# Attention values as 64x64 quarters, in two halves around the next quad's first scores

## The chip, the cores and the metric

The kernel runs on one core of a Trainium2 chip. The metric is device time in microseconds for one execution; the median of several runs is quoted. Beside it there is one profiled execution with its trace. A core has five engines that run their own instruction streams and wait for each other through semaphores: TensorE (PE in the profile; its weight loads are PEld), VectorE (DVE), ScalarE (ACT), GpSimd (POOL) and SyncE (SP), which issues most transfers here.

## The reference

Attention with normalised queries and keys, and then a feed-forward block over its output, all in fp32:

```
q, k, v: (8, 12, 448, 64)
q_n, k_n = rmsnorm(q, g_q), rmsnorm(k, g_k)
scores   = matmul(q_n, k_n^T) / sqrt(64)
attn     = softmax(scores)
x        = matmul(attn, v), laid out as (3584, 768)
h        = x @ w_in                      # 768 -> 1024
solu     = h * softmax(h)
out      = layernorm(solu) * g_ln @ w_out  # 1024 -> 768
```

The weights arrive as float64 and are converted to fp32 in the kernel.

## The kernel before

The work has three stages: attention (to 316 us of the trace), the first product of the feed-forward block, and the second. The change lies in the attention stage, in `fast_path`. `general_path` is a fallback that does not run on these inputs.

**Quads and pairs.** The 96 heads (8 batches of 12) are handled four at a time, as 24 quads; a quad m is two pairs, a = 2m and b = 2m + 1, and a pair is two heads h = 0 and 1 stacked on 128 partitions, 64 each. The 448 keys of a head are three blocks of 128 (kc = 0 to 2) and a rest of 64. Everything is kept transposed: keys on partitions, queries along the free dimension.

**Scores.** `scores(n, kc)` (L804) makes four products of 64x64 weights with 448 columns: two row halves of the array are the two heads, two column halves are the two halves of a key block. The two heads go to two PSUM banks of one tile `s` (pool `ps_t`, tag "t", three buffers of two banks). ScalarE then takes one exponential over both heads (L802), E. `scores_last(m)` (L818) does the rest of 64 keys for both pairs at once. There is no subtraction of a maximum; the gains are bounded by a check instead.

**Values.** Each pair has one PSUM bank `o` (tag "o", two buffers): 64 partitions for each head. `values_last(m)` (L850) begins both banks with the rest of 64 keys, in four products of 64x64: row half i works for pair i. `values(n)` (L863) adds the three key blocks of one pair: 128 keys on all rows of the array, 64 columns for each head, so two products fill the array (shape 128x64). `values(a)` and `values(b)` follow each other. An fp32 product appears in the trace as two matmul instructions.

**Sums and division.** `add` (L836) and `add_more` (L844) add blocks of E on VectorE and GpSimd; `sums(m)` (L874) makes the sums over keys with products against ones, 128x32, into a tile `sm` of tag "t". `inverse(m)` (L896) turns them into reciprocals on VectorE, with copies on GpSimd (L910). `divide(m)` (L912) multiplies `o` by them: two transposes (L917) and two products (L918); the first frees the bank of pair a, the second that of pair b. `store_x` sends the result to DRAM.

**Norms.** For the quad after the next, `squares` (L669, ScalarE) and `row_sums` (L676, VectorE) run; `fold_sums` (L684, GpSimd) joins quarters of partitions. For the next quad, `rsqrt_seed` (L693: L697 and L698 on ScalarE), `rsqrt_step` (VectorE), `normalise` (L709, GpSimd), `qk_transpose` (L720, VectorE) and `gain` (L725, ScalarE, scales q by the gains) prepare `qkT`, which the scores read.

**Weight conversion.** In the quads of `steps_at`, 4 to 10, 12, 14, 16, 18 and 20 (twelve in all), `begin(m)` (L1344) runs the first step of one conversion: `low_bits` (L534), two instructions on ScalarE, of which L536 reads what L535 wrote. `step(m - 1)` runs the second step, on VectorE, one quad later.

**The order.** Inside `manual_schedule` each engine executes its instructions in the order in which the code calls them; the framework adds the semaphore waits. The loop over quads (from L1385) writes that order by hand. `unit(f)` (L1317) calls f and moves a counter on by one unit; `later(n, g)` (L1314) calls g when n more units have passed, so that `divide(m)` is called after the first unit of the next quad. For a quad from 2 to 21 the order on TensorE is: scores of a (three), the last scores, scores of b (three), `values_last`, `values(a)`, `values(b)`, `sums`. On ScalarE: seven exponentials, two squares, two gains, in the quads of `steps_at` L535 and L536, and L697 and L698 for the next norms. The calls behind the last scores read:

```
            if next2:
                squares(a + 4)
                squares(b + 4)
                row_sums(a + 4)
            if next1:
                gain(a + 2)
                gain(b + 2)
```

and, further on, `unit(outputs)` (values_last and values(a)), `step(m - 2)`, `begin(m)`, `step(m - 1)`, loads of weights, and `unit(lambda: values(b))`.

Of the kernel before, what the change touches and what calls it, by code (L numbers as in the profile page):

```python
# [366 lines left out]
def fast_path(  # L367
# [24 lines left out]
    nc = tc.nc  # L392
    B, H, S, D = q.shape
    DM, DFF = moe_w_in.shape
    P = 128
    NJ = S // P
    NB = S // 32
    NP = H // 2
    NQ = B * NP // 2
# [16 lines left out]
    first, middle, banks_in = ExitStack(), ExitStack(), ExitStack()  # L416
# [201 lines left out]
    st = {}  # L618
    quads = {}
# [49 lines left out]
    def squares(n):  # L669
        d = st[n]  # L670
        d["sq"] = work.tile([P, 2 * NB, 32], FP32, tag="sq", name="sq", bufs=2)
        nc.scalar.activation(d["sq"].rearrange("p (s b) d -> p s (b d)", s=2), d["qk"], AF.Square)  # L672
# [20 lines left out]
    def rsqrt_seed(d):  # L693
        ss = d["ss"]
        p, w = ss.shape
        y = d["y"] = small.tile([P, 4 * NB], FP32, tag="ny", name="ny", bufs=2)[0:p, 0:w]
        nc.scalar.activation(y, ss, AF.Ln, scale=1.0 / D, bias=eps[0:p])  # L697
        nc.scalar.activation(y, y, AF.Exp, scale=-0.5)  # L698

    def rsqrt_step(d):  # L700
        y, ss = d["y"], d["ss"]
        p, w = ss.shape
        x = small.tile([P, 4 * NB], FP32, tag="nx", name="nx", bufs=2)[0:p, 0:w]
        nc.vector.tensor_scalar(x, ss, -0.5 / D, -0.5e-6, OP.mult, OP.add)
        nc.vector.tensor_tensor(x, x, y, OP.mult)
        nc.vector.tensor_tensor(x, x, y, OP.mult)
        nc.vector.scalar_tensor_tensor(y, x, 1.5, y, OP.add, OP.mult)
# [17 lines left out]
    def gain(n):  # L725
        d = st[n]
        nc.scalar.activation(d["qkT"][:, 0], d["qkT"][:, 0], AF.Copy, scale=gcol[:, KF : KF + 1])
# [72 lines left out]
    def exponentials(d, kc, s):  # L800
        d["E", kc] = big_tile("E")[:, 0 : 2 * S].rearrange("p (h t) -> p h t", h=2)
        nc.scalar.activation(d["E", kc], s[:, :, 0:S], AF.Exp)  # L802

    def scores(n, kc):  # L804
        d = st[n]
        s = ps_t.tile([P, 2, 512], FP32, tag="t", name="s")

        for c in range(0, P, D):
            for h in range(2):
                hh = slice(h * D, (h + 1) * D)  # L810
                keys = slice(NJ * c + kc, NJ * (c + D - 1) + kc + 1, NJ)
                nc.tensor.matmul(  # L812
                    s[c : c + D, h, 0:S], d["qkT"][hh, 1, keys], d["qkT"][hh, 0, :],
                    start=True, stop=True,
                )
        exponentials(d, kc, s)
# [16 lines left out]
    def on_vector(m):  # L833
        return m >= NQ - 2

    def add(n):  # L836
        d = st[n]
        d["es"] = work.tile([P, 2, S], FP32, tag="es", name="es")
        nc.vector.tensor_tensor(d["es"], d["E", 0], d["E", 1], OP.add)  # L839

    def whole(n):
        return on_vector(n // 2) or n % 2 == 0

# [6 lines left out]
    def values_last(m):  # L850

        d = quads[m]
        for i in range(2):
            o = st[2 * m + i]["o"] = ps_t.tile([P, S], FP32, tag="o", name="o", bufs=2)
        for h in range(2):
            for i in range(2):
                pp = slice(i * D, (i + 1) * D)
                nc.tensor.matmul(  # L858
                    st[2 * m + i]["o"][h * D : (h + 1) * D, :], d["vl"][pp, h], d["E", NJ][pp, h],
                    start=True, stop=False,  # L860
                )

    def values(n):  # L863


        d = st[n]
        for kc in range(NJ):
            for h in range(2):
                nc.tensor.matmul(  # L869
                    d["o"][h * D : (h + 1) * D, :], quads[n // 2]["v"][:, n % 2 + 2 * h, kc], d["E", kc][:, h],  # L870
                    start=False, stop=(kc == NJ - 1),
                )
# [48 lines left out]
    def store_x(m):  # L921
        b, hp = divmod(2 * m, NP)
        xo = quads.pop(m)["xo"]
        rows = xd[b].rearrange("(g h i d) t -> h d g i t", h=2, i=2, d=D)
        for h in range(2):
            nc.sync.dma_start(rows[h][:, hp // 2], xo[h * D : (h + 1) * D])
# [5 lines left out]
    banks = []  # L932
# [384 lines left out]
    def unit(f, steps=4):  # L1317
        nonlocal now
        f()
        now += steps  # L1320
        due = [x for x in todo if x[0] <= now]
        todo[:] = [x for x in todo if x[0] > now]
        for _, g in sorted(due, key=lambda x: x[0]):
            g()
# [40 lines left out]
    with tc.manual_schedule():  # L1365
# [19 lines left out]
        for m in range(NQ):  # L1385
            a, b = 2 * m, 2 * m + 1

            def outputs():
                values_last(m)
                values(a)  # L1390


            next1 = m + 1 < NQ
            next2 = m + 2 < NQ
            next3 = m + 3 < NQ
            early = m > 0 and next1

            def norms_next():
                rsqrt_seed(norms[m + 1])
                rsqrt_step(norms[m + 1])  # L1400
                normalise(a + 2)
                normalise(b + 2)

            if m == 0:
                unit(lambda: scores(a, 0))
                normalise_rows(1, 0)
                normalise_rows(1, 1)
                unit(lambda: scores(a, 1))
                unit(lambda: scores(a, 2))
                squares_half(3, 0, True)  # L1410
                for s in range(2):
                    transpose_rows(1, s)
                    take_rows(1, s)
                squares(2)
                squares_half(3, 1, False)
                add(a)
                add_more(a)
                row_sums(2)
                unit(lambda: scores_last(m))
                row_sums(3)  # L1420
                fold_sums(1)
                unit(lambda: scores(b, 0))
                unit(lambda: scores(b, 1))
                add(b)
                norms_next()
                unit(lambda: scores(b, 2))
                squares(4)
                row_sums(4)
                squares(5)
                unit(outputs)  # L1430
                qk_transpose(2)
                gain(2)
                row_sums(5)
                qk_transpose(3)
                fold_sums(2)
                unit(lambda: values(b))
                unit(lambda: sums(m))
                inverse(m)
                later(1, lambda m=m: divide(m))
                continue  # L1440
            if early:
                norms_next()
            for x in joins_at.get(m, ()):
                combine_in(x)
            if next1:
                load_v(m + 1)
            if m == 1:
                load(m + 3)
            unit(lambda: scores(a, 0))
            if m == 1:  # L1450
                gain(3)
            store_x(m - 1)
            if early:
                qk_transpose(a + 2)
                if next3 and m > 1:
                    load(m + 3)
            unit(lambda: scores(a, 1))
            unit(lambda: scores(a, 2))
            unit(lambda: scores_last(m))
            unit(lambda: scores(b, 0))  # L1460
            unit(lambda: scores(b, 1))
            if early:
                qk_transpose(b + 2)
            add(a)
            if not on_vector(m):
                add_more(a)
            unit(lambda: scores(b, 2))
            if next2:
                squares(a + 4)
                squares(b + 4)  # L1470
                row_sums(a + 4)
            if next1:
                gain(a + 2)
                gain(b + 2)
            if next2:
                row_sums(b + 4)
                fold_sums(m + 2)
            add(b)
            if on_vector(m):
                add_more(a)  # L1480
                add_more(b)
            unit(outputs)
            step(m - 2)
            begin(m)
            step(m - 1)
            if m - 1 in sets:
                load_next()
            if m == 2:
                load_next()
                load_next()  # L1490
            if m == 3:
                norm_gain()
            unit(lambda: values(b))
            if m == NQ - 1:
                block_sums(0, 0)
                block_sums(0, 1)
                load_x(1)
            unit(lambda: sums(m))
            inverse(m)
            if next1:  # L1500
                later(1, lambda m=m: divide(m))
            if m == NQ - 2:
                load_x(0)
                sizes(0)
# [62 lines left out]
        for n in range(NS):  # L1567
            base = period * n
            for i, name in enumerate(ORDER):
# [4 lines left out]
                x = HALVES[name][0]  # L1574
# [118 lines left out]
```

## Time and profile before

| | us |
|---|---|
| runs, median of 3 | 802.53 (802.07 to 803.22) |
| profiled execution, its time | 803.36 |
| span of its trace | 801.6 |
| attention stage, up to the first product of L990 | 316.3 |
| one quad, m = 12 (from values_last to values_last) | 12.52 |
| TensorE busy in 18 to 316 us | 295.92 of 298.00 |
| VectorE, ScalarE, GpSimd busy there | 253.84, 227.26, 214.45 |

The profile's first part gives busy time and share of each engine, the second its share in 40 slices and the granted TensorE clock, the fourth the chain that ended last. A line of the timeline has the start in us, the duration from the first start to the last end, the engine, the source line, the operation, the tile written and those read, the part of the array in rows*columns for products, the shape, the number of merged instructions, and in brackets idle time ahead of it with what ended it. Ends of matmuls are modelled and overlap the next start, so differences of starts tell the pace.

### The profile page before, as it was taken

Reading aid. Unit: us, or ns where it says so; the run is one execution under the profiler, and the core shown is the slowest. Engines: PE = TensorE matmul, PEld = TensorE weight load, DVE = VectorE, ACT = ScalarE, POOL = GpSimd, SP = SyncE. Lnnn points to the kernel's source line nnn. Section 1 sums busy time; section 2 is a strip of 40 time slices with the busy share of each in tenths; the row PEclk is TensorE's granted clock in tenths of the full one; section 3 lists DMA queues with packets and bytes.
Section 4 is the critical chain, followed back from the end, with each engine's and each line's share of the span. In section 5 each row is a group of like instructions: output and inputs, shape, how many; then the busy total and the mean of one; then the engine's idle time right before and its main releaser. Section 6 shows DMA issues by size and latency. Waiting matters only on the chain.

```text
span 801.6 us, 14271 instructions
## 1 busy us (share of the span) xinstructions
PE 788.1 (98%) x4854; PEld 462.7 (58%) x4854; DVE 613.7 (77%) x1202; ACT 472.2 (59%) x783; POOL 523.1 (65%) x664
## 2 busy tenths in 40 slices
PE   8999999999999999999999999999999999999997
PEld 4344444444444443444444444444789999999996
DVE  6787989989888896488878666777896776866945
ACT  6677878878778774376766544444515455464420
POOL 2666777778876784234456467668698777877861
PEclk9999999999999999999999999999999999999999
DMA  9878889897787832445554435552757457366312
GB/s 169 164 174 156 175 194 186 194 189 161 169 157 169 158 102 75 136 117 155 152 146 131 113 98 141 142 137 52 190 167 233 147 183 264 123 221 223 112 61 83
DMA packets 269598, 122.68 MB, mean 153 GB/s; under 512 B 187596, under 2 KB 254668, under 8 KB 269516
## 3 DMA queue, kind: packets, MB, share of 16 engines
q1 hardware_dynamic: 254332, 111.78, 55.9%
q10 hardware_dynamic: 15184, 9.90, 4.5%
q8 instruction: 40, 0.66, 0.3%
q14 instruction: 42, 0.34, 0.1%
HBM read 84.94 MB, written 36.70 MB: 152 GB/s over the span
## 4 chain that ended last, share of the span: by engine, by line
PE 87%; DVE 3%; DMA 2%; SPq 2%; POOL 2%; ACT 2%; issue 1%; DVEq 0%; ACTq 0%; POOLq 0%
PE A L1205 14%; PE A L990 13%; PE o L869 12%; PE s L812 12%; PE B L990 8%; PE B L1205 7%; PE C L990 4%; PE sm L891 4%; PE D L990 4%; PE C L1205 3%; PE s L825 2%; PE o L858 2%; SPq L636 1%; DMA xg<-xd 1%; ACT E L802 1%
## 5 line engine op out<-in xcount | busy, mean ns | idle before, releaser
L802 ACT ACTIVATE E<-s 128x896 f32<-128x896 f32 x168 | 138.8, 937 | 8.3 <-PE s L812 7.8
L812 PE MATMUL s<-qkT 64*64 64x448 f32 x1152 | 120.1, 545 | 1.0 <-ACT qkT L786 0.6
L869 PE MATMUL o<-E,v 128*64 128x448 f32 x576 | 113.8, 543 | 0.0
L1079 POOL TENSOR_TENSOR he<-he,mhalf 128x1 f32<-128x1 f32 x28 | 27.4, 977 | 102.5 <-DVE he L1078 97.4
L812 PEld LDWEIGHTS s<-qkT 64*64 64x64 f32 x1152 | 48.0, 163 | 59.4 <-ACT E L802 29.3
L1205 PE MATMUL A<-w_out,sums 128*128 128x192 f32 x392 | 79.9, 327 | 1.6 <-POOL sums L1185 1.2
L869 PEld LDWEIGHTS o<-E,v 128*64 128x64 f32 x576 | 39.1, 137 | 72.2 <-issue 68.0
L1205 PE MATMUL B<-w_out,sums 128*128 128x192 f32 x392 | 79.8, 326 | 0.5 <-DVE P L1267 0.5
L713 POOL TENSOR_TENSOR qkn<-qk,ny 128x896 f32<-128x896 f32 x46 | 77.2, 1699 | 3.8 <-DMA qk<-in_q_dram 1.5
L848 POOL TENSOR_TENSOR es<-es,E 128x896 f32<-128x896 f32 x22 | 46.4, 2110 | 48.8 <-ACT sq L672 34.0
L990 PE MATMUL B<-w_in,xsum 128*128 128x512 f32 x168 | 76.7, 592 | 0.0
L990 PE MATMUL A<-w_in,xg 128*128 128x512 f32 x168 | 74.6, 593 | 0.0
L1061 ACT ACTIVATE u<-h,hmax 128x1024 f32<-128x1024 f32 x28 | 32.2, 1148 | 66.8 <-DVE hmax L1055 66.8
L1205 PEld LDWEIGHTS A<-w_out,sums 128*128 128x128 f32 x392 | 66.1, 190 | 2.4 <-POOL sums L1185 1.5
L1205 PEld LDWEIGHTS B<-w_out,sums 128*128 128x128 f32 x392 | 66.2, 190 | 0.8 <-DVE P L1267 0.8
L839 DVE TENSOR_TENSOR es<-E 128x896 f32<-128x896 f32 x48 | 53.9, 1124 | 2.7 <-ACT E L802 2.7
L990 PEld LDWEIGHTS B<-w_in,xsum 128*128 128x128 f32 x168 | 31.9, 190 | 40.2 <-issue 39.2
L990 PEld LDWEIGHTS A<-w_in,xg 128*128 128x128 f32 x168 | 31.8, 190 | 40.1 <-issue 39.3
L690 POOL COPY ss<-part 32x56 f32<-32x56 f32 x92 | 47.0, 511 | 5.9 <-DVE part L680 1.4
L680 DVE TENSOR_REDUCE part<-sq 128x28 f32<-128x896 f32 x46 | 47.9, 1080 | 3.9 <-ACT sq L672 1.6
L723 DVE STREAM_TRANSPOSE qkT<-qkn 128x896 f32<-128x896 f32 x46 | 48.4, 1087 | 0.0
L563 POOL TENSOR_TENSOR w_out<-w_out 128x384 f32<-128x384 f32 x44 | 45.0, 1028 | 1.3
(153 smaller groups left out, 1651.0 us busy)
## 6 DMA issues: line engine op xcount, KB each, us to landing
ur<-ud SPq DMA_DIRECT2D x60, 256.0 KB, 4.6
ud<-ub SPq DMA_DIRECT2D x112, 128.0 KB, 2.3
xd<-xo SPq DMA_DIRECT2D x48, 224.0 KB, 3.0
qk<-in_q_dram SPq DMA_DIRECT2D x92, 112.0 KB, 3.1
qk<-in_k_dram SPq DMA_DIRECT2D x92, 112.0 KB, 3.0
v<-in_v_dram SPq DMA_DIRECT2D x24, 384.0 KB, 4.3
out_dram<-P SPq DMA_DIRECT2D x19, 384.0 KB, 4.2
raw<-in_moe_w_in_dram SPq DMA_DIRECT2D x12, 512.0 KB, 5.3
```

What stands on the lines that cost most here:

```text
L563: nc.gpsimd.tensor_tensor(o, p, q, OP.subtract)
L680: nc.vector.tensor_reduce(norms[m]["part"][:, i], st[n]["sq"], AX, OP.add)
L690: e.tensor_copy(ss[g * 32 : g * 32 + 32], part[o * 32 : o * 32 + 32])
L713: e.tensor_tensor(d["qkn"].rearrange("p (s b) d -> p s b d", s=2), d["qk"].rearrange("p s (b d) -> p s b d", d=32), y.rearrange("p (s b) - ...
L723: nc.vector.transpose(d["qkT"].rearrange("p s t -> p (s t)"), d["qkn"].rearrange("p b d -> p (b d)"))
L802: nc.scalar.activation(d["E", kc], s[:, :, 0:S], AF.Exp)
L812: nc.tensor.matmul(s[c : c + D, h, 0:S], d["qkT"][hh, 1, keys], d["qkT"][hh, 0, :], start=True, stop=True,)
L839: nc.vector.tensor_tensor(d["es"], d["E", 0], d["E", 1], OP.add)
L848: e.tensor_tensor(d["es"], d["es"], d["E", 2], OP.add)
L869: nc.tensor.matmul(d["o"][h * D : (h + 1) * D, :], quads[n // 2]["v"][:, n % 2 + 2 * h, kc], d["E", kc][:, h], start=False, stop=(kc == NJ ...
L990: nc.tensor.matmul(k[bank], a[:, c], w_in[i][:, c], start=begin and c == 0, stop=c == HD - 1, skip_group_check=not begin,)
L1205: nc.tensor.matmul(k[bank], a[:, c].rearrange("p a i -> p (a i)"), w_out[:, area, i, c], start=begin and c == 0, stop=c == KC - 1, skip_gr ...
```

## The change

For the quads 1 to 22 (`halved`), the three key blocks of both pairs are multiplied together in 64x64 quarters: of each key block the row half that holds one half of the keys works for pair a while the other works for pair b. `values_part(m, 0)` does this for one assignment of halves to pairs, `values_part(m, 1)` for the exchanged one. [...] `turn(m)` puts a no-op on ScalarE that waits for the last product of part 0, and the first product of part 1 waits for the no-op. Between the two parts stand the next quad's first scores, `scores(a + 2, 0)`, which leave the head of that quad's own order. `gain(a + 2)` is called ahead of the squares, `gain(b + 2)` behind the no-op.

```diff
+    def halved(m):
+        return 0 < m < NQ - 1
+
...
+    def values_part(m, part):
+        first = None
+        for kc in range(NJ):
+            for i in range(2):
+                d = st[2 * m + i]
+                pp = slice((part ^ i) * D, (part ^ i) * D + D)
+                for h in range(2):
+                    x = nc.tensor.matmul(
+                        d["o"][h * D : (h + 1) * D, :], quads[m]["v"][pp, i + 2 * h, kc], d["E", kc][pp, h],
+                        start=False, stop=(part == 1 and kc == NJ - 1),
+                    )
+                    first = first or x
+        if part == 0:
+            quads[m]["half"] = x
+        else:
+            behind(first, quads[m]["turn"])
+
+    def behind(x, y):
+        tc.add_manual_dep(
+            getattr(x, "ins", x), getattr(y, "ins", y).name,
+            mybir.DependencyInfo(mybir.DependencyClass.Sync, mybir.DependencyReason.DATA),
+            reason="row tiles change banks",
+        )
+
+    def turn(m):
+        x = quads[m]["turn"] = nc.scalar.nop()
+        behind(x, quads[m]["half"])
...
             def outputs():
                 values_last(m)
-                values(a)
+                if halved(m):
+                    values_part(m, 0)
+                else:
+                    values(a)
...
-            unit(lambda: scores(a, 0))
             if m == 1:
+                unit(lambda: scores(a, 0))
                 gain(3)
+            else:
+                unit(lambda: scores(a, 1))
             store_x(m - 1)
             if early:
                 qk_transpose(a + 2)
                 if next3 and m > 1:
                     load(m + 3)
-            unit(lambda: scores(a, 1))
+            if m == 1:
+                unit(lambda: scores(a, 1))
             unit(lambda: scores(a, 2))
...
             unit(lambda: scores(b, 2))
+            if next1:
+                gain(a + 2)
             if next2:
                 squares(a + 4)
                 squares(b + 4)
                 row_sums(a + 4)
-            if next1:
-                gain(a + 2)
-                gain(b + 2)
...
-            unit(lambda: values(b))
+            if halved(m):
+                turn(m)
+                gain(b + 2)
+                unit(lambda: scores(a + 2, 0))
+                unit(lambda: values_part(m, 1))
+            else:
+                unit(lambda: values(b))
```

In the changed kernel's instruction streams the no-op stands on ScalarE directly behind L535 and L536 in the quads of `steps_at`, and directly behind the second square in the others (in quad 3 behind a copy of a gain column, L477); the order on VectorE, GpSimd and of SP's transfers is that of before.

## The prediction

> **What bounds the kernel now.** I read the page first. TensorE is busy in nearly every slice at full clock, and the chain that ended last lies on it for 87% of the span: whatever lengthens or shortens TensorE's own sequence in the attention stage moves the end.
>
> ```profile
> PE 788.1 (98%) x4854; PEld 462.7 (58%) x4854; DVE 613.7 (77%) x1202; ACT 472.2 (59%) x783; POOL 523.1 (65%) x664
> PEclk9999999999999999999999999999999999999999
> PE 87%; DVE 3%; DMA 2%; SPq 2%; POOL 2%; ACT 2%; issue 1%; DVEq 0%; ACTq 0%; POOLq 0%
> ```
>
> Then TensorE's timeline of one quad (m = 12; start, duration, line). Quads 1 to 21 repeat it every 12.52 us without idle time, but for quad 3 (12.82, one transpose more).
>
> ```profile
> 165.24 2.52 PE L812 MATMUL s<-qkT 64*64 64x448 f32 x24
> 167.58 0.93 PE L825 MATMUL s<-qkT 64*64 64x448 f32 x8
> 168.33 2.43 PE L812 MATMUL s<-qkT 64*64 64x448 f32 x24
> 170.59 0.93 PE L858 MATMUL o<-E,vl 64*64 64x448 f32 x8
> 171.44 4.73 PE L869 MATMUL o<-E,v 128*64 128x448 f32 x24
> 176.11 0.96 PE L891 MATMUL sm<-E,ones 128*32 128x224 f32 x16
> 176.89 0.94 PE L891 MATMUL sm<-es,ones 128*32 128x224 f32 x16
> 177.76 0.64 PE L812 MATMUL s<-qkT 64*64 64x448 f32 x4
> ```
>
> Read starts, not durations, which overlap. L825 to L812: 0.75 us for eight instructions, which start four together, so 0.376 per filling of the array. The values take 12 steps of two: 12 x 0.376 = 4.51. Both shapes fill the array, and the change wins nothing in products. Where the shape changes, a start comes late: L858 to L869 is 0.86 instead of 0.75 (0.11), L869 to L891 is 4.67 instead of 4.51 (0.16), and L891 and L812 give up the rest, 0.02, 0.11 and 0.08. In the single instructions: 64x64 to 128x64 costs 0.16, 128x64 to 128x32 0.12, 128x32 to 64x64 0.20.
>
> Then ScalarE and VectorE over the same quad, because the change hangs a wait on the one and pulls a product ahead of the other.
>
> ```profile
> 166.32 5.78 ACT L802 ACTIVATE E<-s 128x896 f32<-128x896 f32 x7
> 171.92 1.84 ACT L672 ACTIVATE sq<-qk 128x896 f32<-128x896 f32 x2
> 173.60 1.27 ACT L727 ACTIVATE qkT<-qkT,gcol 128x448 f32<-128x448 f32 x2
> 174.72 0.82 ACT L535 ACTIVATE tmp<-raw,seven 128x512 f32<-128x512 uint32 x1
> 175.57 0.63 ACT L536 ACTIVATE tmp<-tmp 128x512 int32<-128x512 f32 x1
> 177.34 0.34 ACT L697 ACTIVATE ny<-ss,eps 128x56 f32<-128x56 f32 x1 [1.14 <-POOL ss L691]
> ```
>
> From starts: 0.80 per exponential, 0.84 per square, 0.56 per gain, 0.85 from L535 to L536. L536 reads what L535 wrote and waits for its end. Twelve quads (steps_at) have this conversion pair.
>
> ```profile
> 165.38 0.42 DVE L902 STREAM_TRANSPOSE r<-sm 128x224 f32<-128x224 f32 x1 [0.48 <-PE sm L891]
> 169.23 0.62 DVE L918 TENSOR_TENSOR xo<-o,r 128x448 f32<-128x448 f32 x1
> ```
>
> Call t the first score product after the sums (165.24). The second division, which frees the bank of pair b, ends at 169.85 = t + 4.62; L858 needs the bank at t + 5.35. There are 0.73 us to spare.
>
> [...]
>
> ```profile
> 435.74 0.63 ACT L535 ACTIVATE tmp<-raw,seven 128x384 f32<-128x384 uint32 x1
> 436.41 0.52 ACT L536 ACTIVATE tmp<-tmp 128x384 int32<-128x384 f32 x1
> ```
>
> Behind this L536 stands the semaphore wait of L1085, for a VectorE product that ended at 435.39. It ran at 436.412, 6 ns after L536 began, not at 435.4; two more behind L536 (382.35, 396.92) did the same. So the sequencer goes ahead of the engine, but not past an instruction whose own semaphore is missing. The measurement decides.
>
> **The change part by part**, for the 22 quads m = 1 to 22; quads 0 and 23 keep the old form. The order of VectorE, GpSimd and of SP's transfers, compared between the two built programs, is the same; only TensorE's and ScalarE's differ.
>
> *Quarters for values.* Twelve fillings before, twelve after, at 0.376 as L858 shows: nothing. The change of shape into values (0.16) goes; the one into sums stays, now from 64x64, a pair that the trace doesn't have. Bounds: 0.10 to 0.20, the smallest first step and the largest whole switch seen; I take 0.13, near the one into the same 128x32. Saved per quad 0.28 - 0.13 = 0.15 (0.08 to 0.18), in 22 quads **-3.4 us** (-4.0 to -1.8). The quarters are issued with two columns of one row tile together, where L858 alternates rows. L869 also alternates columns at 0.376, so I cost it at nothing[...].
>
> *Squares behind gain(a+2), gain(b+2) behind the no-op.* The first gain starts 0.80 after the last exponential (t + 5.88), ends at t + 6.6, and is needed at t + 7.6. The squares come 0.56 later than they would; the first ends by t + 7.44, and VectorE, busy with the addition at L839 until then, reduces it no sooner than at t + 7.72 today. gain(b+2) and the early exponential take 1.4 us that ScalarE idles through now (1.14 us before L697, 0.87 after it). Nothing. Were that room gone, the price would be what exceeds it.
>
> *One score product pulled ahead.* From t to L858 there are now six score products, not seven: t + 4.60. The division that frees bank b still ends at t + 4.62, since its chain starts at the sums. With 0.05 us from an end on another engine to TensorE (L825 at 306.21 after an exponential that ended at 306.16) and 0.05 until the step is regular again, about 0.1 us is lost (0 to 0.3). The cover of 0.73 is gone. Behind the waiting L858 all values and sums are queued. It counts in the ten quads without conversion, **+1.0**; in the others it is part of the next wait. Quad 2 has its divisions 0.37 us later than the rest: **+0.3**, once.
>
> *The no-op.* The second half may start when the no-op has run, and the no-op needs the first half's end and its turn in ScalarE's order. TensorE reaches the second half at t + 4.60 + 0.75 (L858) + 2.26 (half) + 0.75 (scores) = t + 8.36. In the ten quads without conversion the first half ends at t + 7.8 (last start 7.23, and 0.54), and the answer is back by t + 7.9: hidden by the scores. In the twelve with conversion the no-op stands behind L535 and L536: last exponential at t + 5.08, gain + 0.80, squares + 0.56, L535 after 2 x 0.84 at t + 8.12, L536 and so the no-op at t + 8.97, TensorE at t + 9.05. Wait 0.69, and 0.05 until the step is regular: 0.74 (0.5 to 0.9). Queued behind it: the second half, the sums, the next scores. ScalarE, VectorE and GpSimd fed by them just move with it. 12 x 0.74 = **+8.9 us** (6.0 to 10.8).
>
> Sum: -3.4 + 1.0 + 0.3 + 8.9 = +6.8. The profiled execution (803.36, span 801.6) would become 810.2; it lies 0.8 above the median of the runs. On 802.53 that gives **809.3 us**.
>
> **The rivals.** (A) The above, 809.3; with the ends of its terms 805 to 813. (B) The no-op is not held[...]: only the 0.1 us of bank b stays, in all 22 quads: -3.4 + 2.2 + 0.3, 801.7. [...] against it the three waits behind L536. (C) Faster: the no-op passes, and the bank is free in time because the margin is a few hundredths: -3.4, 799.1. It decides if the no-op runs by t + 8.2 and the division ends by t + 4.55. (D) The issue order of the quarters shows a weight load in each step[...]. For it: L858's rows alternate; against it: L869.
>
> **How the numbers follow.** A 0.80, B 0.09, C 0.06, D 0.05. About 0.2% (1.6 us) is what a measurement can tell from no change: below 800.9 C and a little of B, within it B's rest and A's lowest end, above it A and D: 0.07, 0.10, 0.83. A's own range, 804 to 813, holds 0.75 of all; reaching to B gives 801.5 to 813.0.
>
> **What would show it.** In the new profile: value products at steps of 0.376 in 64x64 form; idle time of TensorE ahead of the second half in the twelve conversion quads alone, about 0.7 us each, ended by ScalarE; their period near 13.1, the others' near 12.45. If the conversion quads show no wait, the no-op overtakes and I am wrong in sign. If all quads wait alike, the round trip over ScalarE is slower than 0.4 us. If steps are above 0.38, D.

## The result and the profile after

The changed kernel takes **808.87 us** (median of four runs, 808.37 to 810.67), beside 802.58 for the kernel before: a ratio of 1.0082, 95% interval 1.0065 to 1.0099. The forecast was 809.3, slower. The profiled execution is the longest of the four, 810.67 with a span of 808.9; that of before was 803.36 and 801.6.

The changed kernel's page first, its busy times and its chain that ended last:

```profile
PE 791.1 (98%) x5382; PEld 494.8 (61%) x5382; DVE 614.2 (76%) x1202; ACT 472.6 (58%) x783; POOL 522.9 (65%) x664
PEclk9999999999999999999999999999999999999999
PE 75%; ACT 9%; DVE 5%; DMA 4%; POOL 2%; issue 2%; SPq 2%; ACTq 0%; DVEq 0%; POOLq 0%
```

The other engines have the same work as before, and TensorE counts more instructions (5382 for 4854: a quarter each for what were halves). What changed is the chain: TensorE had 87% of it and has 75%, and ScalarE 9% instead of 2%. The end now hangs on ScalarE in places. Lines of the file have moved by 33 from L896 on: L861 here is L858 of before, L902 is L869, L924 is L891, L984 is L951. Values in quarters are L875, the no-op is L893.

TensorE's timeline of quads 11 and 12 (start, duration, line; in brackets idle time and what ended it). Quad 11 has no conversion, quad 12 has one:

```profile
162.33 1.05 PE L861 MATMUL o<-E,vl 64*64 64x448 f32 x8
163.08 2.56 PE L875 MATMUL o<-E,v 64*64 64x448 f32 x24
165.33 1.05 PE L812 MATMUL s<-qkT 64*64 64x448 f32 x8
166.09 2.56 PE L875 MATMUL o<-E,v 64*64 64x448 f32 x24
168.57 0.96 PE L924 MATMUL sm<-E,ones 128*32 128x224 f32 x16
...
170.22 1.77 PE L812 MATMUL s<-qkT 64*64 64x448 f32 x16
...
174.82 1.05 PE L861 MATMUL o<-E,vl 64*64 64x448 f32 x8
175.57 2.55 PE L875 MATMUL o<-E,v 64*64 64x448 f32 x24
177.82 1.05 PE L812 MATMUL s<-qkT 64*64 64x448 f32 x8
179.25 2.49 PE L875 MATMUL o<-E,v 64*64 64x448 f32 x24 [0.38 <-ACTq L893]
```

Read the starts. Six fillings in quarters take 2.25 us (163.08 to 165.33), 0.376 each, as in the other shape (171.871 to 172.247 in quad 12 of the kernel before, 128x64). In quad 11 the second half follows the pulled scores after 0.76 us, with no wait. In quad 12 it follows after 1.43, and what ended the wait is L893, the no-op on ScalarE. From `values_last` to `values_last` quad 11 takes 12.49 us and quad 12 13.09; before, both took 12.52.

ScalarE over quad 12 shows why:

```profile
176.11 0.71 ACT L727 ACTIVATE qkT<-qkT,gcol 128x448 f32<-128x448 f32 x1
176.66 1.83 ACT L672 ACTIVATE sq<-qk 128x896 f32<-128x896 f32 x2
178.34 0.80 ACT L535 ACTIVATE tmp<-raw,seven 128x512 f32<-128x512 uint32 x1
179.17 0.63 ACT L536 ACTIVATE tmp<-tmp 128x512 int32<-128x512 f32 x1
```

The no-op stands in the trace at 179.180, 6 ns after L536 began, and TensorE's first weight load of the second half at 179.246. The first half had ended at about 178.1 (ends of matmuls are modelled).

All twelve conversion quads take 13.09 or 13.10 us, the six others from 11 to 21 12.48 or 12.49, quad 1 12.37. Two quads are special: quad 2 took 12.85, and quad 22 14.66 where it took 13.71 before. Against the 12.52 of before the differences add up to 12 x 0.575 (conversion quads) - 6 x 0.035 (the six others) - 0.15 (quad 1) + 0.33 (quad 2) + 0.02 (quad 3, which took 12.82) + 0.95 (quad 22) = 7.8 us to the end of the attention stage. The stages behind it are 0.6 shorter in this profile, for a reason that no run here shows, and the span is 7.3 longer.

### The profile page after: what moved, and what is told of

It is laid out like the page before. It is cut to its first block, busy times and chain, and to the rows that moved or that the text cites. A ratio compares the mean times of both kernels' runs of the same rounds, so it can differ in the third digit from the quotient of the medians.

```text
span 808.9 us, 15350 instructions
## 1 busy us (share of the span) xinstructions
PE 791.1 (98%) x5382; PEld 494.8 (61%) x5382; DVE 614.2 (76%) x1202; ACT 472.6 (58%) x783; POOL 522.9 (65%) x664
## 4 chain that ended last, share of the span: by engine, by line
PE 75%; ACT 9%; DVE 5%; DMA 4%; POOL 2%; issue 2%; SPq 2%; ACTq 0%; DVEq 0%; POOLq 0%
PE A L1238 14%; PE A L1023 13%; PE B L1023 9%; PE o L875 8%; PE B L1238 7%; PE s L812 6%; ACT E L802 5%; PE C L1023 4%; PE D L1023 4%; PE sm L924 4%; PE C L1238 3%; ACT sq L672 2%; DMA v<-in_v_dram 1%; SPq L636 1%; DMA xg<-xd 1%
## 5 line engine op out<-in xcount | busy, mean ns | idle before, releaser
L802 ACT ACTIVATE E<-s 128x896 f32<-128x896 f32 x168 | 141.0, 929 | 15.9 <-PE s L812 15.7
L812 PE MATMUL s<-qkT 64*64 64x448 f32 x1152 | 127.0, 545 | 3.0 <-ACT E L802 2.0
L875 PE MATMUL o<-E,v 64*64 64x448 f32 x1056 | 112.0, 538 | 4.5 <-ACTq L893 4.5
L812 PEld LDWEIGHTS s<-qkT 64*64 64x64 f32 x1152 | 54.5, 163 | 55.6 <-ACT E L802 27.8
L875 PEld LDWEIGHTS o<-E,v 64*64 64x64 f32 x1056 | 58.8, 133 | 46.9 <-issue 15.7
L839 DVE TENSOR_TENSOR es<-E 128x896 f32<-128x896 f32 x48 | 57.3, 1195 | 2.9 <-ACT E L802 2.9
L1238 PE MATMUL A<-w_out,s 128*128 128x192 f32 x224 | 45.6, 326 | 0.0
```

The source lines that it names most:

```text
L812: nc.tensor.matmul(s[c : c + D, h, 0:S], d["qkT"][hh, 1, keys], d["qkT"][hh, 0, :], start=True, stop=True,)
L875: x = nc.tensor.matmul(d["o"][h * D : (h + 1) * D, :], quads[m]["v"][pp, i + 2 * h, kc], d["E", kc][pp, h], start=False, stop=(part == 1 a ...
L1238: nc.tensor.matmul(k[bank], a[:, c].rearrange("p a i -> p (a i)"), w_out[:, area, i, c], start=begin and c == 0, stop=c == KC - 1, skip_gr ...
```

## The experiments

Where an edit is to the changed kernel, it is told as a difference to it. Beside the first four experiments the kernel before had a median of 803.12, beside the last four 803.34, where it had 802.58 beside the changed kernel. So medians of different groups are compared over the kernel before, and a difference of 1 us between them is read from the quads of the profiles.

### The no-op ahead of the conversion

```diff
             unit(outputs)
+            if halved(m):
+                turn(m)
             step(m - 2)
             begin(m)
...
             if halved(m):
-                turn(m)
                 gain(b + 2)
```

> The changed kernel with the no-op called directly behind values_last and the first half, ahead of the conversion steps, so that L535 and L536 stand behind it on ScalarE. Theory (the no-op is held because it stands behind L536, which waits for L535): the wait of TensorE ahead of the second half goes in all twelve conversion quads, whose period falls from 13.09 to about 12.48, that of the other quads: 12 x 0.61 = 7.4 us off 808.9, 801.5. Rival (the exchange of banks itself, or the round trip over ScalarE, costs the time and only happens to be longer there): nothing or little changes, 807 to 809.

Measured: 801.92 us (ratio to before 0.9989, 0.9983 to 0.9996): 1.2 below the kernel before, where the changed kernel was 6.3 above it, so 7.5 less. The second half of quad 12 now follows the pulled scores without a wait:

```profile
173.46 1.05 PE L812 MATMUL s<-qkT 64*64 64x448 f32 x8
174.22 2.56 PE L875 MATMUL o<-E,v 64*64 64x448 f32 x24
```

The twelve conversion quads take 12.48 or 12.49, but for one of 12.55; L535 and L536 run at the same place in the quad as before the edit (3.53 and 4.36 us after `values_last`), and the no-op now at 3.37. So here the exchange of banks and the way over ScalarE cost nothing by themselves: 0.3 us remain between the no-op, at 173.83, and TensorE's need at 174.22, less the 0.07 that the way back took in the changed kernel. The rival falls. Whether the second half has to wait for the first at all was not shown: every kernel here with quarters has the wait.

### The no-op between L535 and L536

```diff
             nc.scalar.activation(low, lo, AF.Relu, scale=-(2.0 ** -29), bias=seven)
+            if between:
+                between.pop()()
             nc.scalar.activation(tmp[:, 1].bitcast(I32), low, AF.Copy, scale=-1.0, bias=7.0)
```

> The changed kernel with the no-op between L535 and L536 in the twelve conversion quads. Theory (ScalarE's sequencer runs ahead of its engine, and is held only by an instruction whose own semaphore is missing, which is L536): L535 has nothing to wait for, the no-op overtakes it, the wait goes, 801.5 as with the no-op ahead of both. Rival (a no-op runs only when all earlier work of its engine is done): it still runs at the end of L535, about 32 ns earlier than now, and the time stays at 808 to 809. If it ran at the start of L535 only, the wait would be gone too, and the place of the no-op in the trace tells that apart from the theory.

What is popped there is `turn(m)`, in the twelve conversion quads; in the others the no-op stays where the changed kernel has it. Measured: 801.93 us (0.9984, 0.9977 to 0.9991). ScalarE in quad 12 of this kernel (L535 is the first of the pair, L538 the second; L674 is the squares):

```profile
172.60 1.83 ACT L674 ACTIVATE sq<-qk 128x896 f32<-128x896 f32 x2
174.28 0.81 ACT L535 ACTIVATE tmp<-raw,seven 128x512 f32<-128x512 uint32 x1
175.13 0.63 ACT L538 ACTIVATE tmp<-tmp 128x512 int32<-128x512 f32 x1
```

`values_last` of this quad starts at 170.755 and the no-op runs 3.364 us later, at 174.119: it is behind L535 in ScalarE's stream, and yet it ran 0.164 us before L535 began (174.283), while the second square was still at work. Behind L536 in the changed kernel it ran only as that one began. So here the busy engine did not hold the no-op, and neither did L535, which merely waited its turn. L536 differs from L535 in that it waits for a semaphore, that of L535's end (in quad 12 of the changed kernel it began at 179.174, 32 ns after that end, where L535 had begun 0.147 us ahead of the end of the square before it, 178.345 and 178.492), and this experiment by itself shows only that it is L536 that holds.

That the missing semaphore is what holds shows in quad 3, where the no-op stands behind another instruction: L477, a copy that waits for a small product of TensorE (L476). All times here are from `values_last` of quad 3. In the kernel with one transpose in the division (its experiment follows below), L476 ended at 3.342, the no-op ran at 3.385, and L477 itself began at 3.523. In the changed kernel the same three times are 3.465, 3.508 and 3.529. So the no-op ran 43 ns after L476 in both, and at no fixed distance from L477's own start, 138 ns ahead of it in the one and 21 in the other. With the no-op called ahead of L477, in the experiment above, it ran at 3.374, before L476 had ended (3.467).

### More work ahead of the conversion

```diff
             if next1:
                 gain(a + 2)
+                gain(b + 2)
             if next2:
                 squares(a + 4)
...
                 turn(m)
-                gain(b + 2)
```

> The changed kernel with gain(b + 2) ahead of the squares too, so that ScalarE reaches L536 later. The second gain waits for the second transpose (176.85 in the new trace, against 176.66 when ScalarE is free), so squares and conversion come 0.8 us later. Theory: the wait in the twelve conversion quads grows by 0.8 each, +9.6, and 1 to 3 us more in the others, because later squares make the next norms and so the divisions late: 819 to 822. Rival (the wait is not set by ScalarE's queue): 809 to 812, the late norms alone.

Measured: 820.13 us (1.0203, 1.0186 to 1.0221). The quad's second half on TensorE in quad 12:

```profile
183.22 1.03 PE L812 MATMUL s<-qkT 64*64 64x448 f32 x8
185.44 2.49 PE L875 MATMUL o<-E,v 64*64 64x448 f32 x24 [1.19 <-ACTq L893]
```

The idle time counted there is 1.19 us, from 0.38. The no-op comes 5.11 us (5.15 in the later quads) after `values_last` instead of 4.37, and the conversion quads take 13.83 to 13.88; the others 12.75. For the twelve and the six others from 11 to 21 that makes 12 x 0.76 + 6 x 0.27 = 10.7; over the kernel before, the medians differ by 17.0 - 6.3 = 10.7 too. The wait follows ScalarE's queue one to one: no-op and period move by the same 0.74 to 0.79. It also prices the place of `gain(b + 2)`. In quad 12 L536 begins 0.79 us later than in the changed kernel: the second gain itself takes 0.56, and it waits about 0.17 for the second transpose on VectorE, which ends at 182.29.

### One transpose in the division

```diff
+        r = work.tile([P, 2 * NB, 32], FP32, tag="r", name="r", bufs=1)
+        nc.vector.transpose(r, quads[m]["rc"].rearrange("p i t b -> p (i t b) ()").to_broadcast([P, 2 * NB, 32]))
         for i in range(2):
             n = 2 * m + i
-            r = work.tile([P, NB, 32], FP32, tag="r", name="r", bufs=1)
-            nc.vector.transpose(r, quads[m]["rc"][:, i].rearrange("p t b -> p (t b) ()").to_broadcast([P, NB, 32]))
-            nc.vector.tensor_tensor(xo[:, i], st[n]["o"], r.rearrange("d b i -> d (b i)"), OP.mult)
+            nc.vector.tensor_tensor(
+                xo[:, i], st[n]["o"], r[:, i * NB : (i + 1) * NB].rearrange("d b i -> d (b i)"), OP.mult
+            )
             del st[n]
```

> The changed kernel with one transpose of 128x896 in divide for both pairs in place of two of 128x448, so that the second division ends about 0.28 us earlier against the sums. Theory (values_last waits about 0.12 us for the bank of pair b in all halved quads, but in the conversion quads the later wait swallows it): the quads without conversion go from 12.48 to 12.37, the twelve stay at 13.09; with quad 2, 1.1 to 1.4 us off: 807.6. Rival (the wait for the bank counts everywhere): 22 x 0.12 = 2.7 off, 806.2. Rival (there is no such wait): 808.9.

Measured: 807.81 us (1.0053, 1.0040 to 1.0067): 4.7 above the kernel before, where the changed kernel was 6.3 above it. The two medians are of few runs (six and four) and can't tell the expected 1.1 to 1.4 from the 2.7 of the first rival; the quads can. The same quad 11 as above, in this kernel:

```profile
161.66 0.93 PE L861 MATMUL o<-E,vl 64*64 64x448 f32 x8
162.41 2.43 PE L875 MATMUL o<-E,v 64*64 64x448 f32 x24
164.67 0.93 PE L812 MATMUL s<-qkT 64*64 64x448 f32 x8
165.42 2.43 PE L875 MATMUL o<-E,v 64*64 64x448 f32 x24
167.78 0.96 PE L924 MATMUL sm<-E,ones 128*32 128x224 f32 x16
```

From the second half to the sums it is 2.36 us, where it was 2.48. The difference of 0.12 is the wait for pair b's bank, but it is not where one would look: no start of a group is late in the kernel with it. Only the durations tell, 1.05 and 2.56 instead of 0.93 and 2.43. In the single instructions of quad 11 the first quarter of each step starts in time and the other three later, by 0.08 us in the first step of `values_last` and by 0.13 from the second on (the second quarter is pair b's: the division that frees the bank ended at 162.352, its weight load began at 162.404, and the other two follow it by 7 and 14 ns). That distance stays to the last of the sixteen steps, through the values and the scores, until the change of shape for the sums closes it. Quads 11 to 21 without conversion take 12.36 or 12.37, those with conversion 13.08 or 13.09, and quad 2 12.51: the wait counts only where no later one swallows it, as the forecast put it. The sum of these is 1.2 us; quad 22, at 13.96, is another 0.7 shorter in this profile.

### Both repairs

The edits of the first and the fourth experiment together.

> The changed kernel with both repairs: the no-op ahead of the conversion steps, and one transpose in divide for both pairs. Theory: neither wait is left, all quads from 4 to 21 run at 12.37, which is 12.52 less the 0.15 of the one shape change saved, and the whole comes to 2.5 to 3.5 us under the kernel before, 799.6 where that is 802.6. Rival (the saved shape change is worth nothing, and the quarters only move time about): 802 to 803.

Measured: **799.1 us** (0.9940, 0.9928 to 0.9953), faster than the kernel before and than the changed one. All quads from 4 to 21 take 12.37; this is quad 12, a conversion quad, from `values_last` to `values_last`:

```profile
169.53 0.93 PE L861 MATMUL o<-E,vl 64*64 64x448 f32 x8
...
181.90 0.93 PE L861 MATMUL o<-E,vl 64*64 64x448 f32 x8
```

The one change of shape is worth 0.15 us in each. But 22 x 0.15 is 3.3, the profiled spans differ by 2.6, and the medians by 4.2, more than the 2.5 to 3.5 expected: where the rest comes from was not shown.

### The division's transpose in the kernel before

The edit of the fourth experiment, to the kernel before.

> The kernel before, with one transpose in divide for both pairs and nothing else. Theory: VectorE's faster division is hidden there, since the bank of pair b is free 0.73 us ahead of values_last: quads at 12.52 and no change, 0.997 to 1.002 of before. Rival (a shorter division helps by itself): 1 us or more faster.

Measured: 803.18 us beside 803.34 (0.9999, 0.9991 to 1.0007), quads at 12.52, though the second division now ends 1.07 us ahead of the need instead of 0.73 (seen at quad 22). In these runs the shorter division was worth something only where the pulled scores had taken its cover: 0.12 us a quad in the changed kernel, nothing here.

### The new order with the old shape

The edit of the fourth experiment, and with it:

```diff
             def outputs():
                 values_last(m)
-                if halved(m):
-                    values_part(m, 0)
-                else:
-                    values(a)
+                values(a)
...
             if halved(m):
-                turn(m)
                 gain(b + 2)
                 unit(lambda: scores(a + 2, 0))
-                unit(lambda: values_part(m, 1))
+                unit(lambda: values(b))
```

> The order of the kernel with both repairs (the next quad's first scores between two parts of the values, one transpose in divide), but the values of pair a and of pair b as the kernel before has them, 128x64, without exchange and without no-op. Theory (what the quarters save is the changes of shape, and each costs what the kernel before showed, 0.12 to 0.20): per quad 0.16 + 0.20 + 0.16 + 0.12 + 0.20 = 0.84 of changes against 0.33 in quarters: 12.88 a quad, 22 x 0.51 = 11.2 over the kernel with both repairs, 810.8. Rival (the order makes the gain, not the shape): within 1 us of that kernel.

Measured: 810.43 us (1.0079, 1.0063 to 1.0096); most quads 12.86, where 12.88 was expected. TensorE in quad 12 of this kernel:

```profile
174.55 0.93 PE L861 MATMUL o<-E,vl 64*64 64x448 f32 x8
175.41 2.48 PE L902 MATMUL o<-E,v 128*64 128x448 f32 x12
177.82 1.01 PE L812 MATMUL s<-qkT 64*64 64x448 f32 x8
178.76 2.48 PE L902 MATMUL o<-E,v 128*64 128x448 f32 x12
```

Six fillings from 175.41 to 177.82 take 2.41 us where quarters take 2.25, and two of scores 0.94 where they take 0.75. In this quad each group in another shape than the one ahead of it starts late: by 0.11 us at 175.41, 0.15 at 177.82, 0.19 at 178.76, and 0.15 at the sums, which start at 181.17. With the old shape this order takes 11.3 us more than with quarters, and 7.1 more than the kernel before; the shape makes the gain.

### The first load of the next stage, earlier

The edits of both repairs, and with them:

```diff
+            if m == NQ - 2:
+                load_x(0)
             store_x(m - 1)
...
             if m == NQ - 2:
-                load_x(0)
                 sizes(0)
```

> The kernel with both repairs and the first load of the feed-forward stage (load_x(0)) issued ahead of the store of quad 21 in quad 22. Theory (the longer quad 22 of all kernels with the pulled scores comes from that transfer, issued behind a store that waits for the divisions, and ScalarE holds the exponentials behind squares of what it brings): quad 22 falls from about 14 to 12.7 us, 1 to 1.5 us off the kernel with both repairs. Rival (the transfer's landing is set by the memory, not by its issue): no change.

Measured: 798.57 us (0.9938, 0.9925 to 0.9951). The profiles agree with the theory: quad 22 falls from 14.34 to 12.22 us. ScalarE at that place in the kernel with both repairs (L986 is L951 of the kernel before, the squares of what the load brings):

```profile
297.21 0.92 ACT L802 ACTIVATE E<-s 128x896 f32<-128x896 f32 x1
302.33 0.84 ACT L986 ACTIVATE xsum<-xg 128x768 f32<-128x768 f32 x1 [4.21 <-DMA xg<-xd]
```

and in this one, the same two lines:

```profile
296.98 0.92 ACT L802 ACTIVATE E<-s 128x896 f32<-128x896 f32 x1
297.79 0.83 ACT L986 ACTIVATE xsum<-xg 128x768 f32<-128x768 f32 x1
```

The squares no longer wait 4.21 us for the transfer, and so the exponentials behind them don't either. But the medians differ by 0.5 only, not by the 2.1 of the profiles or the 1 to 1.5 expected, and their intervals against before overlap. The profiled execution of the kernel with both repairs was its longest, 800.71; whether the other executions had the wait in full was not measured. This one stays inconclusive beyond the shift seen in the trace.

## Why the prediction was right

**Quarters.** Put at a saving of 0.15 a quad, and at nothing for the products: the kernel with both repairs shows 12.37 for 12.52, so 0.15, and 0.376 a step. (22 x 0.15 is 3.3, not the forecast's 3.4, and the upper ends of its terms add up to 815, not 813; neither touches the result.) The pair of shapes that the trace of before lacked, 64x64 to 128x32, was taken at 0.13; it measures 0.103 to 0.111 at its first step and 0.024 at its second.

**Squares behind gain(a + 2).** Costed at nothing; the quads without a wait show nothing.

**The score product pulled ahead.** Put at 0.1 in each of ten quads, 0.3 more in quad 2. Against the quads without a wait it is 0.12 in the six from 11 to 21 (12.49 for 12.37), 0.13 in quad 3, and 0.48 in quad 2 (12.85 for 12.37); quad 1 has none. Quad 22, the tenth, can't be read for it. These nine make 1.3, as the forecast had for its ten.

**The no-op.** The forecast had it at t + 8.97, t being the first score product after the sums. In quad 12 t is 170.22, and the no-op ran at 179.18, t + 8.96. The period of a conversion quad was forecast at 13.1 and measures 13.09. The reason given was that the sequencer is held by an instruction whose own semaphore is missing. It had only three semaphore waits behind L536 for it, in another stage, which could not tell a missing semaphore from the mere start of L536; the no-op between L535 and L536, which ran 0.164 us before L535 began, shows that the sequencer ran ahead of the engine, and quad 3, where it ran 43 ns after L476's end in both kernels, that it was the semaphore that held.

**The rivals.** B and C, that the no-op is not held, had no trace to speak for them; they fall with 0.67 us of late second halves in each of the twelve quads. C is also near what the repaired kernel became, by the two conditions that the forecast named for it; that both say 799.1 is chance, since C stood 3.4 below the kernel before and the repaired kernel 4.2. D falls with the step of 0.376: the weight loads of the quarters took 0.133 us each (median of L875) and did not lengthen it.

**What was missing.** The sum left out quad 22, 0.95 longer in the profile. SP's order was found the same, and the forecast stopped there. But its load for the next stage stands behind a store that waits for quad 21's divisions. The load was issued at 304.04, 1.3 us after `values_last`, where it had been 0.6 before, because the divisions now stand later against the values; and it took 8.1 us to land instead of 7.1. ScalarE's squares wait for it, the exponentials behind them, and TensorE for these. The same order on a queue is not the same time. Only the later issue, 0.75 us, is laid to the change: the kernel before with one transpose issued this load 0.24 us after `values_last` and it took 7.7 us to land, with 14.02 us for quad 22; in the other kernels that issue it here it took 7.7 to 8.1. So the 7.1 of before may be chance, and a part of the 0.95 with it.

**Where luck came in.** Quads 1 to 21 add up to 6.9 us longer, beside the 6.8 of the forecast's sum, and that is not luck. That the missing 0.95 of quad 22 doesn't show in the total is: the stages behind were 0.6 shorter, and the profiled execution lies 1.8 above its median where that of before lies 0.8 above, so that the spans differ by 7.3 and the medians by 6.3.

## What to carry to other kernels

Here the synchronisation over ScalarE cost its place in that engine's stream: 0.67 us a quad behind L536, which waits for a semaphore, nothing ahead of L535 or between the two. So look not at how busy the engine is there, but at which instructions ahead of the synchronisation still wait for a semaphore, one of the engine's own included, and put the no-op ahead of the first of them. When work is moved from in front of a deadline to behind it, recompute every chain that is anchored at the start of that stretch; a division that had 0.73 us to spare had none, and a transfer behind it was issued 0.75 us late.

## What the runs showed of the hardware

- ScalarE's sequencer ran a semaphore instruction 0.16 us before the activation that stands ahead of it in the stream had begun (174.119 and 174.283, quad 12 with the no-op between L535 and L536); behind an activation that waits for the one before it, it ran 6 ns after that one's start (179.180 and 179.174, quad 12 of the changed kernel); behind one that waits for TensorE, it ran 43 ns after the modelled end of TensorE's product (3.508 and 3.465 in quad 3 of the changed kernel, 3.385 and 3.342 with one transpose), and in the second of these 0.14 us before that activation began (3.385 and 3.523).
- Quarters of TensorE ran out of step. Three that were held back behind the first, by 0.08 us in the first step and 0.13 from the second on, kept that distance to the last of sixteen steps, with no idle time counted, until the next change of shape (quad 11 of the changed kernel).
- The path PE to ScalarE's no-op and back took about 0.13 us in the changed kernel, with a modelled end of the products in it: in quad 11 the last products of the first half end at 165.64, the no-op ran at 165.70, and in the waiting quads TensorE's weight load followed the no-op's start by 0.066 (179.180 and 179.246 in quad 12).
- A change of shape cost 0.12 to 0.20 us in quad 12 of the kernel before; the pair that its trace lacked, 64x64 to 128x32, cost about 0.13 in quad 12 of the changed kernel, the lateness of its first two steps together (0.110 and 0.024).
